# Three staged warming matmuls, and the first w1 loads on ScalarE's queue, in a fused attention and token-mixing kernel

## The chip, the cores and the metric

The kernel runs on one core of a Trainium2 chip. The metric is the time of one execution on the device, in microseconds (us). A kernel is executed several times, and executions of the kernel before are interleaved with those of the other kernel on the same chip. Every execution here counts as the normal ("fast") state. The profile is that of one execution. Its span runs from the first to the last instruction and is about 1.8 us shorter than the time.

## The reference, cut to what matters

```python
x = A_x                                    # 2048 tokens x 1024, bf16
xn = layernorm(x)
out = x + A_ref(xn, ...) + B_ref(xn, ...)  # A_ref: attention with memory, not touched here

def B_ref(x, w1, b1, w2, b2):              # mixes tokens
    h = layernorm(x)
    u = gelu(einsum('bsd,sf->bdf', h, w1) + b1)    # contracts over the 2048 tokens
    return (einsum('bdf,fs->bds', u, w2) + b2).transpose(0, 2, 1)
```

The tokens are cut into 16 blocks of 128. Token block c of h meets row block c of w1, so the first matmuls need x block 0 (normalised) and w1's row block 0, and nothing more.

## The kernel before: the parts that matter

The kernel records each operation with what it reads and writes, and derives semaphore waits from that. The rule: a write waits for every earlier *reader* of the same record.

```python
def _waits(self, es, reads, writes, extra=()):       # cut
    for r in reads:
        add(r.w)                                     # wait for the last writer
    for r in writes:
        add(r.w)                                     # (with one exception, cut)
        for t in r.r.values():
            add(t)                                   # ... and for all readers since
    for t in extra:
        add(t)
```

The head of the kernel loads x and w1 on one queue (SyncE's, "SP") and issues ten matmuls on zeroes, which are only there to get TensorE's clock up:

```python
for kind, c0, n in (("x", 0, 1), ("x", 1, 1), ("x", 2, 1), ("w", 0, 2), ("x", 3, 1), ("x", 4, 2), ("w", 2, 2), ...):
    ...                                              # n blocks from block c0 on, one DMA each
with fw.group(reads=[self.R_warm], writes=[self.R_bank[0]]):
    for _ in range(self.N_WARM):                     # N_WARM = 10
        fw.mm(self.bank(0), self.warm[:, 0:P], self.warm[:], start=True, stop=True)
```

Then the blocks are normalised in the order of a small script. `D`/`d` are statistics on VectorE (DVE; a small d does half a block), `A` statistics on ScalarE (ACT), `S` the variance step (DVE, then a pow on GpSimd, POOL), `h` the scaling on DVE that makes h.

```python
NORM_ORDER = (["D0 A1 S0 d2 h0 A1' A3 S1 d2' h1"] + ...)

def rstd(self, c):                                   # "S"
    R, var, rs = self.R_st[c], self.ln_mv[:, c, 1:2], self.ln_rs[:, c, 1:2]
    fw.op("dve", lambda e: e.tensor_scalar(var, ...), reads=[R], writes=[R])
    fw.op("pool", lambda e: e.tensor_tensor(rs, var, self.expo[:, 0:1], op=ALU.pow), reads=[R, self.R_expo], writes=[self.R_rs[c]])
```

`early_hidden` follows: for each block, 8 matmuls (4 groups of 128 of w1's columns times 2 halves of h).

The softmax here doesn't subtract the row's maximum and nothing guards it: scores larger than these inputs give would overflow.

## Time and profile before

| | before |
|---|---|
| time, median of 3 at first (of 6 with those run beside the change) | 697.68 us (697.53) |
| span of the profiled execution | 695.4 us |
| TensorE busy | 685.7 us, 99% |
| first real matmul | 7.09 us |
| x block 0 / x block 2 / w1 blocks 0 and 1 landed | 3.57 / 5.91 / 6.73 us |
| granted clock recorded as rising at | 5.84 us |

A transfer has landed when its semaphore reaches its full count; those times are read from the trace's semaphore records. In the views PE is TensorE, PEld its weight loads, L194 line 194 of the kernel, and a q after an engine's name (SPq) is its instruction queue. First, part 1 of the page of the kernel before, and the first line of part 4 (shares of the chain of waits):

```profile
span 695.4 us, 11228 instructions
PE 685.7 (99%) x4746; PEld 326.5 (47%) x4830; DVE 257.2 (37%) x581; ACT 277.7 (40%) x333; POOL 100.4 (14%) x156
...
PE 97%; DMA 1%; issue 1%; SPq 1%; DVE 0%
```

Then the wait view of TensorE over the whole span (waiter, releaser: total us, number, longest us):

```profile
PE ps_all L194 <- DVE h L656: 1.4, 1, 1.4
PE ps_all L194 <- DVE brow L517: 1.3, 1, 1.3
PE ps_all L194 <- issue: 0.3, 2, 0.2
```

The 1.3 us are the wait for the zeroes at the very start. There is almost nothing left to wait for. A change of the head can only move the moment at which real matmuls begin, or the clock at which the first of them run. The timeline of the head shows how that moment comes about (columns: start, duration, engine, line, operation; in brackets the idle time before it and who ended it):

```profile
1.25 4.45 PE L194 MATMUL ps_all<-warm 128*128 128x512 bf16 x10 [1.25 <-DVE brow L517]
...
3.59 1.42 DVE L617 BATCH_NORM_STATS2 ln_st<-xin 128x6 f32<-128x512 bf16 x2 [2.35 <-DMA xin<-in_A_x_dram]
...
5.29 0.15 DVE L639 TENSOR_SCALAR ln_mv<-ln_mv 128x1 f32<-128x1 f32 x1
...
5.53 0.55 POOL L641 TENSOR_TENSOR ln_rs<-ln_mv,expo 128x1 f32<-128x1 f32 x1 [3.96 <-DVE ln_mv L639]
...
5.94 0.69 DVE L617 BATCH_NORM_STATS2 ln_st<-xin 128x6 f32<-128x512 bf16 x1 [0.49 <-DMA xin<-in_A_x_dram]
...
6.55 0.72 DVE L656 TENSOR_SCALAR h<-xin,ln_mv,ln_rs 128x512 bf16<-128x512 bf16 x2
...
7.09 11.17 PE L194 MATMUL ps_all<-h,w1early 128*128 128x512 bf16 x50 [1.39 <-DVE h L656]
```

The pow for block 0 is done at 6.08, but h starts only at 6.55. DVE was in between busy with the statistics of block 2, which stand before h in its order and which had waited 0.49 us for that x block. TensorE was idle from 5.70 to 7.09. The warming matmuls are 0.43 us apart and the first real ones 0.216 us, so the clock doubled in between.

### The profile page before, as it was taken

How to read it: one execution, taken by the hardware profiler on the slowest of the kernel's cores; microseconds unless marked ns; L12 is line 12 of the kernel's file. 1: busy time of each engine (PE TensorE's matmuls, PEld its weight loads, DVE VectorE, ACT ScalarE, POOL GpSimd, SP SyncE). 2: the span in 40 equal slices, each digit the busy share in tenths (PEclk: the TensorE clock that was granted, in tenths of full speed). 3: DMA queues.
4: the chain of work that ended last, by engine and by line, in shares of the span. 5: the costliest groups of instructions: out<-in, count | busy, mean ns of one | idle time of the engine just before them, and what ended most of it. 6: DMA issues, size and time to landing. Idle time of an engine off the chain costs nothing.

```text
span 695.4 us, 11228 instructions
## 1 busy us (share of the span) xinstructions
PE 685.7 (99%) x4746; PEld 326.5 (47%) x4830; DVE 257.2 (37%) x581; ACT 277.7 (40%) x333; POOL 100.4 (14%) x156
## 2 busy tenths in 40 slices
PE   8999999999999999999999999999999999999998
PEld 3444444444444444444444445444444444445454
DVE  7740000000011334333436455536445553434445
ACT  7521211111134444444455444454544444534440
POOL 2600000000001111111121211112121111121130
PEclk9999999999999999999999999999999999999999
DMA  9497684227036536645263544525273544437014
GB/s 315 110 218 175 151 224 123 77 60 140 1 133 121 109 67 131 115 109 126 47 129 95 117 95 90 129 47 137 64 150 80 97 95 73 97 64 152 9 31 137
DMA packets 210537, 77.17 MB, mean 111 GB/s; under 512 B 173112, under 2 KB 202808, under 8 KB 210488
## 3 DMA queue, kind: packets, MB, share of 16 engines
q1 hardware_dynamic: 210344, 76.42, 47.8%
q8 instruction: 38, 0.62, 0.4%
q14 instruction: 11, 0.09, 0.1%
q10 hardware_dynamic: 144, 0.03, 0.0%
HBM read 59.79 MB, written 5.24 MB: 94 GB/s over the span
## 4 chain that ended last, share of the span: by engine, by line
PE 97%; DMA 1%; issue 1%; SPq 1%; DVE 0%
PE ps_all L194 97%; DMA xin<-in_A_x_dram 1%; SPq L216 1%; DVE ln_st L617 0%; DVE fin L1051 0%; PE ps_all L200 0%
## 5 line engine op out<-in xcount | busy, mean ns | idle before, releaser
L194 PE MATMUL ps_all<-gT,w2h 128*128 128x512 bf16 x868 | 207.8, 380 | 1.6 <-issue 0.2
L811 ACT ACTIVATE pT<-ps_all 128x512 bf16<-128x512 f32 (+1 forms) x128 | 151.4, 1234 | 76.7 <-PE ps_all L194 76.7
L194 PE MATMUL ps_all<-h,w1s 128*128 128x512 bf16 x752 | 165.1, 379 | 0.8
L806 POOL TENSOR_SCALAR_AFFINE_SELECT pT<-pT 128x512 bf16<-128x512 bf16 x128 | 83.9, 680 | 557.5 <-ACT pT L811 557.5
L194 PEld LDWEIGHTS ps_all<-gT,w2h 128*128 128x128 bf16 x896 | 83.1, 98 | 105.7 <-issue 13.8
L194 PEld LDWEIGHTS ps_all<-h,w1s 128*128 128x128 bf16 x768 | 75.1, 98 | 90.6
L845 DVE CAST ost<-ps_all 128x264 bf16<-128x264 f32 (+1 forms) x128 | 49.2, 398 | 169.4 <-PE ps_all L194 169.3
L713 ACT ACTIVATE gT<-ps_all,b1c 128x512 bf16<-128x512 f32 x56 | 35.1, 687 | 142.0 <-PE ps_all L194 136.4
L755 DVE CAST kT<-ps_all 128x512 bf16<-128x512 f32 x32 | 22.0, 688 | 176.9 <-PE ps_all L194 176.9
L194 PE MATMUL ps_all<-xnT,wk 128*128 128x512 bf16 x256 | 60.5, 379 | 0.0
L194 PE MATMUL ps_all<-xnT,wq 128*128 128x512 bf16 x256 | 60.4, 378 | 0.0
L194 PEld LDWEIGHTS ps_all<-vA,pT 128*128 128x128 bf16 x1280 | 47.7, 96 | 22.6
L194 PE MATMUL ps_all<-wv_sb,xnT 128*128 128x512 bf16 x227 | 54.0, 379 | 1.6
L739 ACT ACTIVATE qT<-ps_all 128x512 bf16<-128x512 f32 x32 | 19.1, 597 | 77.8 <-PE ps_all L194 77.8
L194 PE MATMUL ps_all<-vA,pT 128*128 128x33 bf16 x1280 | 48.6, 178 | 0.0
L951 DVE SCALAR_TENSOR_TENSOR stg<-ps_all,b2c,stg 128x512 bf16<-128x512 f32 x32 | 24.0, 750 | 61.7 <-PE ps_all L194 61.6
L758 ACT ACTIVATE etmp<-kT 128x512 bf16<-128x512 bf16 x24 | 15.1, 629 | 59.0 <-DVE kT L755 59.0
L194 PEld LDWEIGHTS ps_all<-xnT,wk 128*128 128x128 bf16 x256 | 23.8, 98 | 23.1
L194 PEld LDWEIGHTS ps_all<-wv_sb,xnT 128*128 128x128 bf16 x256 | 23.5, 97 | 23.7
L194 PEld LDWEIGHTS ps_all<-xnT,wq 128*128 128x128 bf16 x256 | 23.4, 97 | 23.2
L773 ACT ACTIVATE vA<-ps_all 128x512 bf16<-128x512 f32 x32 | 19.2, 600 | 37.1 <-PE ps_all L194 37.1
L194 PE MATMUL ps_all<-qT,kT 32*128 32x384 bf16 (+3 forms) x512 | 31.9, 299 | 0.0
(70 smaller groups left out, 419.7 us busy)
## 6 DMA issues: line engine op xcount, KB each, us to landing
w2h<-in_B_w_dram SPq DMA_DIRECT2D x32, 448.0 KB, 4.8
w1s<-in_B_w_dram SPq DMA_DIRECT2D x12, 1024.0 KB, 5.8
wq<-in_A_wq_dram SPq DMA_DIRECT2D x32, 256.0 KB, 4.4
wk<-in_A_wk_dram SPq DMA_DIRECT2D x32, 256.0 KB, 5.1
stg<-in_A_x_dram SPq DMA_DIRECT2D x16, 256.0 KB, 3.0
out_dram<-stg SPq DMA_DIRECT2D x16, 256.0 KB, 2.0
xin<-in_A_x_dram SPq DMA_DIRECT2D x2, 1024.0 KB, 10.5
wv_sb<-in_A_wv_dram SPq DMA_DIRECT2D x2, 1024.0 KB, 9.0
```

Of the source, the lines that this page charges most:

```text
L194: ins = self.nc.tensor.matmul(*args, **kwargs)
L216: ins = es.eng.dma_start(out_ap, in_ap, transpose=True) if transpose else es.eng.dma_start(out_ap, in_ap)
L713: fw.op("act", lambda e: e.activation(self.gT[:, fc, half * 512:(half + 1) * 512], self.bank(b), ACT.Gelu_apprx_tanh, bias=self.b1c[:, fc: ...
L739: fw.op("act", lambda e: e.activation(self.qT[k][:], self.bank(b), ACT.Copy), reads=[self.R_bank[b]], writes=[self.R_qT[k]])
L755: fw.op("dve", lambda e: e.tensor_copy(self.kT[k][:], self.bank(b)), reads=[self.R_bank[b]], writes=[self.R_kT[k]])
L758: fw.op("act", lambda e: e.activation(self.etmp[1][:], self.kT[k][:], ACT.Exp), reads=[self.R_kT[k]], writes=[self.R_etmp[1]])
L773: fw.op("act", lambda e: e.activation(self.vA[i][:, c, :, 0:D_HEAD], self.bank(b).rearrange("p (h d) -> p h d", d=D_HEAD), ACT.Copy), read ...
L806: fw.op("pool", lambda e: e.affine_select(d, d, pattern=[[0, 4], [1, P]], compare_op=ALU.is_ge, fill=0.0, base=0, channel_multiplier=-1), ...
L811: self.fw.op("act", lambda e: e.activation(dst, src, ACT.Exp, scale=SCALE), reads=R_src, writes=R_dst)
L845: fw.op("dve", lambda e: e.tensor_copy(dst, self.ps[:, b, 0:n * VW]), reads=[self.R_bank[b]], writes=[self.R_ost[o][qb]])
L951: fw.op("dve", lambda e: e.scalar_tensor_tensor(dst, self.bank(b), self.b2c[:, c:c + 1], dst, op0=ALU.add, op1=ALU.add), reads=[self.R_ban ...
```

## The change

The intent: bridge the idle stretch with three more warming matmuls, staged to start once block 0's statistics are there, so that the clock stays up; and get w1's first blocks earlier by letting ScalarE's queue issue them, while SyncE's queue goes on with x.

```diff
-        for kind, c0, n in (("x", 0, 1), ("x", 1, 1), ("x", 2, 1), ("w", 0, 2), ("x", 3, 1), ("x", 4, 2), ("w", 2, 2), ("x", 6, 2),
-                            ("w", 4, 4), ("x", 8, 4), ("w", 8, 4), ("x", 12, 4), ("w", 12, 4)):
+        for kind, c0, n in (("x", 0, 1), ("x", 1, 1), ("w", 0, 2), ("x", 2, 1), ("w", 2, 2), ("x", 3, 1), ("x", 4, 2),
+                            ("x", 6, 2), ("w", 4, 4), ("x", 8, 4), ("w", 8, 4), ("x", 12, 4), ("w", 12, 4)):
...
-                            writes=self.R_w1e[c0:c0 + n])
+                            writes=self.R_w1e[c0:c0 + n], issuer="act" if c0 < 4 else "sp")
...
-        with fw.group(reads=[self.R_warm], writes=[self.R_bank[0]]):
-            for _ in range(self.N_WARM):
+        self.keep_warm(self.N_WARM)
+
+    def keep_warm(self, n, reads=()):
+        fw = self.fw
+        with fw.group(reads=[self.R_warm, *reads], writes=[self.R_bank[0]]):
+            for _ in range(n):
                 fw.mm(self.bank(0), self.warm[:, 0:P], self.warm[:], start=True, stop=True)
...
-    NORM_ORDER = (["D0 A1 S0 d2 h0 A1' A3 S1 d2' h1"] +
+    NORM_ORDER = (["D0 W0 A1 S0 d2 h0 A1' A3 S1 d2' h1"] +
...
+            elif kind == "W":
+                self.keep_warm(3, [self.R_st[c]])
```

`W0` *reads* the record of block 0's statistics, and `S0`, two steps on, *writes* it.

## The prediction

> **What bounds the kernel.** TensorE is busy 685.7 of 695.4 us (part 1 of the page) and holds 97% of the chain of waits. The wait view lists two TensorE waits of size: 1.3 us at the start, for the memsets, and 1.4 us before the first real matmul, ended by DVE's h. After that matmul starts at 7.09 us TensorE waits only 0.3 us more. So the change can move the time by the shift of that start, plus the clock in the first microseconds; nothing later absorbs it.
>
> **The start (timeline).** x block 0 lands at 3.57 us. DVE's statistics run 3.59 to 5.26, the variance step 5.29, POOL's pow 5.53 to 6.08, h's first half 6.55 to about 6.9, the matmul 7.09. h waited about 0.4 us behind DVE's next statistics, which waited 0.49 us for x block 2 (landed 5.91). w1's pair 0 landed at 6.73. The ten warming matmuls are 0.43 us apart (cold), the last ends at 5.70; the granted-clock record rises at 5.84, and the first real matmuls are 0.216 us apart: already warm.
>
> **What the change does.**
> 1. Queue: ScalarE issues the two w1 loads after its table load and dummy activation, at about 2.3 us; pair 0 was issued at 2.19, pair 2 at 3.65. ScalarE was idle until 4.19, so two issues of 0.45 us are free. The sync queue issues x blocks 3 to 7 about 0.5 to 1 us sooner, but the DMA engines are over 90% busy from 2 us on. The Trainium skill ("DMA: Bandwidth & Descriptors", "Issuing engines are not separate DMA queues") says that both queues share the same 16 engines; no run yet shows it here. I expect w1 pair 0 up to 0.7 us earlier, x blocks 0 to 2 at most 0.4 us later: -0.2 to +0.2 us by itself.
> 2. Warming: the three matmuls follow block 0's statistics and sit behind the ten, so they run from 5.5 us, 0.43 us each, or less once the clock rises, and fill most of the gap. No bubble of work is removed; in the profiled run the clock was up in time anyway. "TensorE: Matmul & The Clock Gate", part 1, calls the activity window free-running, so other executions may start cold; the times before spread from 697.3 to 699.26, which would fit. There the added matmuls may save up to 1 us.
> 3. The hidden cost: the warming group reads block 0's statistics record, and DVE's variance step writes it. The built program shows that step now waiting on TensorE's semaphore, which it did not before. So it starts not at 5.29 but when the third warming matmul is done: 6.5 us if the clock rises at 5.84, 7.0 if all are cold. Then +0.88 us to h (as for later blocks), +0.54 to the matmul: 8.0 to 8.45 us instead of 7.09. Loss 0.9 to 1.35 us, all critical. The next statistics fit into the pow's wait.
>
> **Sum.** +1.1 us from the wait, 0 from the queues, -0.3 on average from a warmer clock: 698.4 us, 80% range 697.0 to 699.8. Faster by over 2%: 0.01; within 2%: 0.98; slower by over 2%: 0.01.
>
> **What would show it.** First real matmul at 8.0 to 8.5 us; DVE's variance step of block 0 at 6.5 to 7.1, released by TensorE; a TensorE gap of about 1.5 us after the third warming matmul; w1 pair 0 landed before 6.7; no other TensorE wait; first real matmuls 0.216 us apart.
>
> **What would make it wrong.** Most executions before starting cold, so that warming wins over 1 us; x block 0 delayed by the second queue; a later TensorE wait for an x block.

## The result, and the profile after

Ratios here are the mean time of one kernel's fast runs over that of the other's of the same rounds, so not quite the ratio of the medians quoted.

| | before | after |
|---|---|---|
| median of 6 runs | 697.53 us (697.14 to 699.26) | 698.03 us (697.77 to 700.39) |
| ratio, 95% interval | | 1.0010 (0.9992 to 1.0029) |
| repeated later (11 and 6 runs), medians | 697.54 us | 698.58 us |
| ratio there | | 1.0015 (1.0000 to 1.0031) |
| span profiled | 695.4 us | 696.0 us |
| first real matmul | 7.09 us | 7.70 us |

This is no change within 2%, and it leans to slower by 0.1%. (The repeat ran on chip 14, e1 to e8 below on chip 15.) The wait view of TensorE in the changed kernel:

```profile
PE ps_all L194 <- DVE h L662: 1.6, 1, 1.6
PE ps_all L194 <- DVE brow L517: 1.3, 1, 1.3
PE ps_all L194 <- issue: 0.2, 1, 0.2
```

The timeline of its head:

```profile
1.24 0.98 ACTq L216 DMA_DIRECT2D w1early<-in_B_w_dram  x2
...
1.25 4.86 PE L194 MATMUL ps_all<-warm 128*128 128x512 bf16 x13 [1.25 <-DVE brow L517]
...
3.58 1.42 DVE L623 BATCH_NORM_STATS2 ln_st<-xin 128x6 f32<-128x512 bf16 x2 [2.33 <-DMA xin<-in_A_x_dram]
...
6.24 0.15 DVE L645 TENSOR_SCALAR ln_mv<-ln_mv 128x1 f32<-128x1 f32 x1 [1.00 <-PE ps_all L194]
6.31 0.68 DVE L623 BATCH_NORM_STATS2 ln_st<-xin 128x6 f32<-128x512 bf16 x1
6.48 0.55 POOL L647 TENSOR_TENSOR ln_rs<-ln_mv,expo 128x1 f32<-128x1 f32 x1 [4.91 <-DVE ln_mv L645]
...
7.14 0.73 DVE L662 TENSOR_SCALAR h<-xin,ln_mv,ln_rs 128x512 bf16<-128x512 bf16 x2
...
7.70 4.48 PE L194 MATMUL ps_all<-h,w1early 128*128 128x512 bf16 x20 [1.58 <-DVE h L662]
```

And its chain of waits for the head, in order of time:

```profile
1.26 4.88 PE ps_all L194 x13
...
6.24 0.17 DVE ln_mv L645
...
6.48 0.56 POOL ln_rs L647
...
7.14 0.42 DVE h L662
...
7.70 7.93 PE ps_all L194 x36
```

Read the last two together. DVE finished block 0's statistics at 5.24 and then stood still for 1.00 us until TensorE, the engine that is waiting for DVE, had finished its *warming* matmuls. TensorE is idle for 1.58 us in place of 1.39: the stretch that was to be bridged has only moved. The real matmuls begin 0.61 us later, and the span is 0.6 us longer. Nothing later absorbs it: 4000 weight loads further on the changed kernel is still 0.61 us behind (572.98 against 572.37).

### The profile page after: what moved, and what is told of

It is laid out like the page before. It is cut to its first block, busy times and chain, and to the rows that moved or that the text cites. A ratio compares the mean times of both kernels' runs of the same rounds, so it can differ in the third digit from the quotient of the medians.

```text
span 696.0 us, 11235 instructions
## 1 busy us (share of the span) xinstructions
PE 686.2 (99%) x4749; PEld 326.7 (47%) x4833; DVE 257.2 (37%) x581; ACT 277.6 (40%) x333; POOL 100.1 (14%) x156
## 3 DMA queue, kind: packets, MB, share of 16 engines
HBM read 59.79 MB, written 5.24 MB: 93 GB/s over the span
## 4 chain that ended last, share of the span: by engine, by line
PE 99%; issue 1%; DVE 0%; POOL 0%; DVEq 0%
PE ps_all L194 99%; POOL ln_rs L647 0%; DVE h L662 0%; DVE fin L1057 0%; DVE warm L515 0%; PE ps_all L200 0%; DVE ln_mv L645 0%; DVE brow L517 0%; DVEq L69 0%
```

## The experiments

Twelve runs were made, of ten new kernels and of the two old ones once more; all were correct. The theories were:

- **A.** The recorded read is the loss: DVE's variance step waits for TensorE.
- **B** (rival to A). The second queue with its new load order, or TensorE's occupation by the warming matmuls, is the loss.
- **C.** Staged warming could gain something, because in some executions the idle stretch costs a period at half clock. **D** (rival to C): that is chance, and three matmuls do not move it.

### Each half alone, and the record alone

**e1**: the changed kernel, but the staged group waits without being recorded as a reader:

```diff
-        with fw.group(reads=[self.R_warm, *reads], writes=[self.R_bank[0]]):
+        with fw.group(reads=[self.R_warm], writes=[self.R_bank[0]], extra=[r.w for r in reads]):
```

> The changed kernel with one thing undone: the three warming matmuls still wait for block 0's statistics and still run, but are not recorded as readers of them, so DVE's variance step need not wait for TensorE. Theory A (the recorded read is the whole loss): the variance step starts at about 5.3 us instead of 6.24; DVE's next statistics then wait for x block 2 (landed 6.04 in the changed kernel), h starts at about 6.7 and the first real matmul at 7.2 to 7.3 instead of 7.70; span about 0.45 us shorter than the changed kernel. Rival B (the matmuls' own occupation of TensorE, or the second queue's contention, is the loss): variance step early or not, the first real matmul stays near 7.7.

**e2**: the changed kernel without the staged group (`W0` struck out of the order).

> The new load order and ScalarE's queue alone, no staged warming matmuls. Theory A: as e1_norecord, first real matmul at 7.2 to 7.3 us, 0.1 to 0.2 later than before, because x block 2 lands about 0.1 us later; w1 pair 0 lands near 5.1 instead of 6.73 and is not waited for. Rival B (queue contention is the loss): first real matmul near 7.7.

**e3**: the staged group, recorded, with the load order and single queue of before.

> The three staged warming matmuls alone (recorded as readers), with the load order and the single queue of before. Theory A: the variance step waits for TensorE and starts at 6.2 us (clock up near 5.0) to 7.1 us (all cold), first real matmul 7.7 to 8.5; span 0.6 to 1.35 us over before. Rival B (the queue is the loss): first real matmul near 7.1 us as before.

**e4**: e1 with `h0` before `d2`: `"D0 W0 A1 S0 h0 d2 A1' A3 S1 d2' h1"`.

> e1_norecord with DVE's h of block 0 put before the statistics of block 2. Theory A plus its second part (without the recorded read, what holds h back is the statistics of block 2 that stand before it in DVE's order and wait for that x block): variance step 5.3, pow to 6.1, h at about 6.15, first real matmul 6.6 to 6.8 us; span about 0.4 us under before and 1.0 under the changed kernel. If instead something else holds the start, the first real matmul stays at 7.1 us or later.

Measured (11 runs of before in the same rounds have a mean of 697.61 us; the ratios are to them):

| | variance step | x block 2 landed | first real matmul | mean time | ratio (95%) |
|---|---|---|---|---|---|
| e1 | 5.16 | 6.63 | 7.81 | 698.83 | 1.0022 (1.0007 to 1.0037) |
| e2 | 5.14 | 6.42 | 7.60 | 698.77 | 1.0018 (1.0003 to 1.0033) |
| e3 | 6.53 | 5.53 | 7.99 | 698.16 | 1.0009 (0.9997 to 1.0021) |
| e4 | 5.06 | 7.48 | 6.52 | 697.42 | 0.9999 (0.9987 to 1.0011) |

Theory A is half right. In e3, where only the staged group is present, DVE's timeline shows its wait for TensorE:

```profile
6.53 0.15 DVE L645 TENSOR_SCALAR ln_mv<-ln_mv 128x1 f32<-128x1 f32 x1 [1.39 <-PE ps_all L194]
```

The first real matmul is at 7.99, 0.90 us later than before. So the recorded read alone moves the start by the low end of what was predicted (0.9 to 1.35 us); the mean time rose by 0.55 us, and the interval of its ratio contains 1. But e1, which undoes just that in the changed kernel, gained nothing: it expected 7.2 to 7.3 and got 7.81. The chain of waits of e1 says why:

```profile
1.72 4.91 DMA xin<-in_A_x_dram
...
6.66 0.04 DVE ln_st L623
...
7.27 0.41 DVE h L662
...
7.81 8.36 PE ps_all L194 x38
```

With the false wait gone, the statistics of block 2 are next in front of h, and their x block landed only at 6.63. e2 has no staged matmuls at all and shows the same: 6.42, and a first real matmul at 7.60. So rival B is right about the loads. x block 2 landed at 5.29 to 6.18 us in the eight that have the load order of before on a single queue, and at 5.93 to 7.48 in the five with ScalarE's queue (after twice, e1, e2, e4). In exchange w1's blocks 0 and 1 landed at 4.94 to 5.48 where they had landed at 6.56 to 7.09. The transfer that got earlier was not the one that h waited for. Queue and order were never parted: e7 below, with a single queue but one w1 block ahead of x block 2, had that x block at 6.27.

The two delays lie side by side, not one after the other. The traces let this be worked out. The first real matmul comes 1.46 us after the variance step where that step holds h (after, e3, e4, e10), and 1.18 us after x block 2's landing where that does (before, e1, e2, e5, e8). For the changed kernel these give 6.24 + 1.46 = 7.70 and 6.04 + 1.18 = 7.22, and in its second profile (e10) 8.47 and 7.11: the later one counts, and it is the recorded read. Had x block 2 landed in e1 as early as in the changed kernel, e1 would have started at about 7.2, as it expected. It landed 0.59 us later instead. Each kernel has one or two profiles, so whether that was chance is not known.

e4 tests the last part: with h in front of block 2's statistics, h no longer cares about x block 2. The first real matmul came at 6.52, as expected, although x block 2 landed as late as 7.48. Here that landing comes back one block later (TensorE's timeline in e4):

```profile
6.52 1.89 PE L194 MATMUL ps_all<-h,w1early 128*128 128x512 bf16 x8
9.50 3.68 PE L194 MATMUL ps_all<-h,w1early 128*128 128x512 bf16 x16 [1.09 <-DVE h L662]
```

The 0.57 us won at the start were paid back with 1.09 us in the profiled execution. Over five executions the mean is level with before.

### The clock

Times of e1 and e2 are worse than their first matmuls explain: the means are 1.2 us over before, with three of six executions each 1.5 us or more above the kernel's lowest. The profile of e2 happened to fall on such an execution. TensorE's timeline in e2 has a long idle stretch in front of the first real matmul:

```profile
1.25 4.32 PE L194 MATMUL ps_all<-warm 128*128 128x512 bf16 x10 [1.25 <-DVE brow L517]
7.60 1.66 PE L194 MATMUL ps_all<-h,w1early 128*128 128x512 bf16 x6 [2.03 <-DVE h L662]
```

This is the table of e2 by stretches of time, the columns being the stretch, its length, then busy time with the number of instructions for PE, PEld, DVE, ACT and POOL, then the granted clock, the DMA share and GB/s:

```profile
5.00:8.00 3.00, 0.97 (x4) 0.22 (x3) 1.81 (x7) 2.02 (x4) 0.63 (x2) 1.00 0.99 330
8.00:9.00 1.00, 1.00 (x5) 0.40 (x4) 0.97 (x4) 0.66 (x1) 0.47 (x1) 0.86 1.03 351
9.00:12.00 3.00, 3.00 (x8) 1.03 (x7) 2.48 (x8) 2.87 (x6) 1.10 (x2) 0.50 1.07 390
12.00:13.00 1.00, 1.00 (x6) 0.47 (x5) 0.95 (x3) 0.97 (x1) 0.55 (x1) 0.93 1.06 389
```

Between 9 and 12 us TensorE is busy all the time but gets through 8 matmuls at a clock of 0.50; the kernel before has 15 in the same stretch. The clock records behind this say: up at 5.31, down at 8.72, up at 12.13. Each of the two stretches is 3.413 us long. The first of them contains the 2.03 us of idling between the last warming matmul and the first real one (5.57 to 7.60). The Trainium skill, "TensorE: Matmul & The Clock Gate", part 1, "What's actually happening", describes a free-running window of 3413 ns in which the activity is judged. This trace agrees on the length, to the nanosecond; and in the profiles of before, after and e8 the clock stayed up for 689.492, 692.906 and 686.079 us, which are 202, 203 and 201 such periods. A period of 3.413 us at half clock costs half of it, about 1.7 us (an estimate).

So the idle stretch before the first real matmul can, it seems, cost more than its own length. Three kernels with staged matmuls on a single queue, and one with fewer warming matmuls, tested that.

**e5**: the staged group without the record (e3 with the edit of e1).

> The three staged warming matmuls alone, on the loads and single queue of before, waiting for block 0's statistics but not recorded as readers. Theory C (what the staged matmuls are good for is that they shorten TensorE's idle stretch, which in some executions costs one 3.41 us window at half clock; the recorded read and the second queue each undo that): variance step at 5.2 to 5.3 us, x block 2 landed 5.5 to 5.9, first real matmul 6.9 to 7.1, idle before it 0.2 to 0.8 us; no execution at a granted clock of 0.998 or less; mean of the fast runs 0.2 to 0.5 us under before because before's executions at 698.6 and over become rare. Rival D (the clock state of an execution is chance that three matmuls do not move): the same share of executions, a quarter to a third, is 1.3 us or more above the lowest.

**e6**: e5 with `h0` before `d2`.

> As e5_warm_norecord, with DVE's h of block 0 put before the statistics of block 2. Theory A, second part: h starts at about 6.1 instead of 6.5 us and the first real matmul is set by w1 pair 0's landing (6.6 to 6.7) at 6.7 to 6.9 us, 0.2 to 0.3 under before; block 1's h comes later, so TensorE may wait 0.1 to 0.4 us for it at 8.5 us. Net gain 0 to 0.3 us on e5_warm_norecord. If x block 2 did not matter: first real matmul as in e5_warm_norecord.

**e7**: e6 with the order `"D0 W0 A1 S0 h0 A1' A3 S1 d2 h1 d2'"` and w1's blocks 0 and 1 loaded apart: `("x", 0, 1), ("x", 1, 1), ("w", 0, 1), ("x", 2, 1), ("w", 1, 1), ("x", 3, 1), ...`.

> A version meant to beat both: single queue, w1's block 0 and block 1 loaded apart (the first matmuls need block 0 alone), staged warming without the record, h of blocks 0 and 1 before the statistics of blocks 2 and 3. Expected: w1 block 0 landed by 5.6 us, h of block 0 at 6.1, first real matmul 6.5 to 6.7 us against 7.09, no second TensorE wait, no execution at a lowered clock; span about 0.5 us under before's 695.4, mean of the fast runs 0.6 to 1.0 us under before. If h of block 1 or x block 2 comes late instead, a second TensorE wait for DVE's h shows before 12 us.

**e8**: the kernel before with `N_WARM = 6`.

> The kernel before with six warming matmuls instead of ten: the idle stretch before the first real matmul grows from 1.4 to about 3.2 us, nothing else changes. Theory C: the first real matmul still at 7.1 us, but real matmuls 0.43 us apart for 1.5 to 6 us in most executions, so most run 0.7 to 3 us above before's lowest; mean of the fast runs 1 to 2 us over before. Rival D: same as before within 0.3 us.

Measured (12 runs of before, mean 697.69; 11 of them are those listed beside e1 to e4, so this comparison is mostly with runs of an earlier call on the same chip):

| | first real matmul | idle before it | times | ratio (95%) |
|---|---|---|---|---|
| e5 | 7.36 | 1.30 | 697.33 to 697.48 (4 runs) | 0.9999 (0.9984 to 1.0013) |
| e6 | 6.65 | none | 697.11 to 697.48 (4 runs) | 0.9997 (0.9982 to 1.0011) |
| e7 | 6.77 | 0.51 | 697.89 to 698.16 (4 runs) | 1.0007 (0.9994 to 1.0020) |
| e8 | 7.08 | 3.09 | 698.51 to 699.86 (4 runs) | 1.0024 (1.0011 to 1.0037) |

e8 is the clear one. The first real matmul starts where it did (7.08), and yet every execution is longer than before's median of 697.49. A line of the table of e8, with the same columns, shows again 8 matmuls in 3 us:

```profile
9.00:12.00 3.00, 3.00 (x8) 1.06 (x7) 2.83 (x10) 2.88 (x5) 1.10 (x2) 1.00 1.07 391
```

A caution for reading: the clock column says 1.00 here because the first clock record of this trace is the rise at 12.53, and what lies before the first record is shown as full speed. The spacing of the matmuls tells the truth: 0.43 us until then. So 5.45 us of back-to-back real matmuls ran at half clock. e8 thus shows what too little warming costs, with a clock that had not been up before; a fall of the clock after idling is shown by e2 alone.

e5 shows the other side. Its first matmul is not earlier than before's (the expected 6.9 to 7.1 was missed, because x block 2 landed at 6.18 in the profiled execution), and its idle stretch of 1.30 us is hardly shorter than the 1.39 of before, but its four executions lie within 0.15 us. e6 adds the order and starts at 6.65.

e7, which was meant to beat everything, missed. The early start was given back to a later wait, on block 2:

```profile
6.77 3.61 PE L194 MATMUL ps_all<-h,w1early 128*128 128x512 bf16 x16 [0.51 <-DVE h L662]
11.27 9.01 PE L194 MATMUL ps_all<-h,w1early 128*128 128x512 bf16 x41 [0.88 <-DVE ln_mv L645]
```

### A last comparison on another chip

**e9**: e6's loads with e7's order. **e10**: the changed kernel again. **e11**: the kernel before with `N_WARM = 13`, nothing staged. **e12**: the kernel before again.

> e6_warm_norecord_hfirst with its loads kept and DVE's order of e7_best (variance step of block 1 before the statistics of block 2, h of block 1 before the second half of them). In e6 TensorE waited 0.2 us for h of block 1; in e7 the gain was given back by a 0.88 us wait for block 2, behind x blocks 4 and 5, which landed at 9.96 instead of 8.95. With e6's loads: first real matmul 6.6 to 6.7 us, no wait for block 1, none over 0.1 us for block 2; mean 0.1 to 0.3 us under e6's 697.26. If the order itself is what delays block 2, a TensorE wait of 0.3 us or more shows between 10 and 11.5 us and the mean is not under e6's.

> The changed kernel, unaltered, once more, beside the others. Theory C: first real matmul 7.6 to 8.4 us, idle stretch 1.4 us or more before it; median 698.0 to 698.7 us, and of six executions one to three at a granted clock of 0.998 or less and 1.3 us or more above its lowest. Rival D: no such executions, or as many in the other three kernels of this call.

> The kernel before with 13 warming matmuls in the one ungated group instead of 10, nothing staged. Theory C: the same as e5_warm_norecord: first real matmul 7.0 to 7.4 us, set by DVE's h, idle before it 1.3 us or less, all executions within 0.5 us of each other, median 697.2 to 697.5; staging buys nothing over a longer plain group. If the staging itself matters, executions 1.3 us above the lowest appear as in before.

> The kernel before, unaltered, for a second profile. Theory C: first real matmul 7.0 to 7.3 us; a quarter to a half of the executions 1.2 us or more above the lowest; if the profiled one is of these, its real matmuls start 0.43 us apart and the clock record rises after 8 us; if it is not, they start 0.216 us apart.

Measured (11 further runs of before in the same rounds: median 697.54, mean 698.02):

| | first real matmul | median (range) | ratio (95%) |
|---|---|---|---|
| e9 | 6.86 | 697.45 (697.36 to 697.61) | 0.9994 (0.9981 to 1.0007) |
| e10, after | 8.47 | 698.58 (698.20 to 700.58) | 1.0015 (1.0000 to 1.0031) |
| e11 | 7.14 | 697.24 (697.08 to 697.66) | 0.9992 (0.9979 to 1.0005) |
| e12, before | 6.64 | 697.61 (696.91 to 698.96) | 0.9998 (0.9984 to 1.0012) |

The second profile of the changed kernel (e10) has the wait for TensorE at its full size, since the clock was late and all thirteen matmuls ran slowly:

```profile
7.01 0.15 DVE L645 TENSOR_SCALAR ln_mv<-ln_mv 128x1 f32<-128x1 f32 x1 [1.78 <-PE ps_all L194]
```

Its first real matmul is at 8.47, a little beyond the 7.6 to 8.4 that had been expected of this run. The second profile of before (e12) shows the head at its best: x block 2 had landed at 5.29, DVE had no wait in front of h, and only w1's blocks 0 and 1 (6.58) held the first matmul:

```profile
6.64 13.71 PE L194 MATMUL ps_all<-h,w1early 128*128 128x512 bf16 x61 [1.17 <-DMA w1early<-in_B_w_dram]
```

The head of one and the same kernel thus varies by 0.45 us with the landing of x block 2.

e11 is a change of one number and does what the change was meant to do: it fills most of the idle stretch. TensorE's timeline in e11 (what held the first real matmul there was w1's pair of blocks, landed at 7.09):

```profile
1.25 5.51 PE L194 MATMUL ps_all<-warm 128*128 128x512 bf16 x13 [1.25 <-DVE brow L517]
7.14 2.12 PE L194 MATMUL ps_all<-h,w1early 128*128 128x512 bf16 x9 [0.37 <-DVE ln_mv L639]
```

It was to have all its executions within 0.5 us and has them within 0.58. e9 missed its size: no gain on e6, and a 0.48 us wait for block 2 shows that the order of e7, and not only its loads, delays that block.

The executions that lie 1.2 us or more above the lowest of their kernel in their call, counted over everything:

| | long executions |
|---|---|
| before | 2 of 6, 4 of 12, 5 of 11, and 2 of 6 as e12 |
| after | 2 of 6, and 1 of 6 as e10 |
| e1, e2 (second queue) | 3 of 6 each |
| e3 (recorded staging), e4 | 0 of 5 each |
| e8 (six warming matmuls) | 2 of 4, and all 4 above 698.5 us |
| e5, e6, e7, e9, e11 | 0 of 4, 0 of 4, 0 of 4, 0 of 5, 0 of 5 |

13 of 35 executions of before are long, and none of the 22 of the five kernels in the last row, all of which keep one queue and issue thirteen warming matmuls that hold nobody up. If both groups were equally prone to them and the executions independent, such a split would come up about 6 times in 10,000. The long executions are thus not chance that three matmuls leave unmoved: rival D falls.

What stays open: where exactly the limit lies, and whether a shorter idle stretch or the longer warming in front of it is what helps (the changed kernel and e1 also issue thirteen and still had long executions). e1 and e5 issue the same warming matmuls and had 1.23 and 1.30 us of idling in their profiled executions, but e1 had three long executions of six and e5 none of four, a difference that so few executions can show by chance. The stretch differs between executions with the landing of x block 2, and apart from e8's only one profile (e2) caught a long execution. Long executions of before, some of them with a recorded clock of 1.0, were never caught; that they are of the same kind (clock up late, or down again for one period) is likely from e2 and e8, not shown. Nor is it shown that e6, e9 or e11 is faster than before: all their intervals contain 1.

## Why the prediction was right or wrong

The time was predicted as 698.4 us (697.0 to 699.8) and measured as 698.03, and 698.58 in the repeat. The range also holds the time of before (697.68), so the time alone confirms little; the timeline has to. Point by point:

- **Only the start of the real matmuls counts, and nothing absorbs it: right.** First matmul +0.61 us, span +0.6 us.
- **The recorded read makes DVE wait for TensorE: right**, with the mechanism as said. The variance step started at 6.24 (predicted 6.5 to 7.1) and 7.01 in the second profile; the first real matmul at 7.70 (predicted 8.0 to 8.45) and 8.47. Both fell short of their ranges in the first profile, and that has its reason in the clock, which rose at 5.00 in that execution in place of 5.84. Alone (e3) the read costs 0.90 us, the low end of what was predicted.
- **"-0.2 to +0.2 us by itself" for the queue: wrong.** Alone (e2) it moved the first matmul from 7.09 to 7.60, because x block 2 landed at 6.42, and the mean by +0.18%, about 1.2 us (part of it the clock, as in the profile of e2). "x blocks 0 to 2 at most 0.4 us later" held for block 2 in the changed kernel (6.04 against 5.91) but not in e1, e2 and e4. That the time came out right in spite of it is in part luck: in the two profiles of the changed kernel the path through x block 2 would have ended at 7.22 and 7.11, before that of the read (7.70 and 8.47), and hid behind it.
- **"-0.3 on average from a warmer clock": not there.** The false wait opened a new idle stretch of 1.58 us, longer than the old one, and 3 of 12 executions were still long. What e5, e6 and e11 show is that the long executions can be made to vanish (none of 13), not that the mean is shorter.
- **w1's pair 0 before 6.7: right** (5.06), but this was not what h or TensorE waited for. That ScalarE would issue at 2.3 us was wrong: its queue issued at 1.24, during its own table load.
- **No other TensorE wait; first real matmuls 0.216 us apart: right** in the profiled executions.

The two wrong terms (a queue that costs, a clock gain that is not there) changed the sum little: the read hid the first, and the second was small.

## What to carry to other kernels

When a filler operation must only *follow* something, make it wait for it without recording a read: a read puts it in the way of the next writer, and here that was the step the whole core was waiting for. Before a load is moved to a second queue, ask which landing holds the critical operation: here the DMA engines were over 90% busy from 2 us on, and when w1's first blocks came one to two us earlier, x block 2 came later. A delay that lies beside another delay shows only when the other is gone, so undo parts of a change one by one before adding up their costs; and a plain group of warming matmuls only has to be long enough: in this kernel four warming matmuls fewer (e8) cost 1.5 us in the mean (699.20 against 697.69), and three more (e11) cost nothing measurable.

## What the Trainium skill lacked or had wrong

- "TensorE: Matmul & The Clock Gate", part 1: its table gives an idle window of about 3.4 us as the cause of a fall to half clock, and its practical rules speak of gaps over 3 us. In e2 a stretch of 2.03 us of idling inside one recorded period of 3.413 us was followed by a period at 0.50. Idling for part of a period sufficed in this trace, and 1.58 us within one period (after, profiled) did not do it.
- The same page says that what is issued in the first ~3.4 us runs at half clock and everything after at full clock. In e8 the clock stayed down for 5.45 us of back-to-back matmuls (7.08 to 12.53), after six earlier warming matmuls. That does not fit the budget, but it fits the page's own free-running window: counted back from the rise, the period from 9.12 to 12.53 is the first that lies wholly behind the start of the real matmuls, and the one before it had 1.38 us of idling.
- "DMA: Bandwidth & Descriptors", "Issuing engines are not separate DMA queues": it fits that a second queue gives no bandwidth (the same bytes, up to x blocks 8 to 11, had landed at 14.42 to 15.59 us in the five profiles with it and at 14.95 to 15.60 in the eight with the old order and a single queue). But it says that this only saves issue time. Here, together with the new order, it also changed who lands first: w1's pair 0 at 4.94 to 5.48 in place of 6.56 to 7.09 us, x block 2 at 5.93 to 7.48 in place of 5.29 to 6.18. The arbitration between rows described in "Queues, rings and completion order" of that page could do this; no run here isolates it from the new order.
- No page says outright that a DMA start placed behind a table load and an activation on ScalarE can leave before they are done, though what the skill says of the sequencer lets one infer it: the start was issued at 1.24 us, while the table load ran from 0.80 to 2.08.
